# An attention and long-convolution kernel: the multiply that ends a head group goes from VectorE to GpSimd, and the table of scheduling rules is written anew

## The chip, the cores and the metric

The kernel runs on one core of one Trainium2 chip. A core has TensorE (PE, matrix multiply), VectorE (DVE), ScalarE (ACT), GpSimd (POOL) and SyncE (SP, which only issues transfers); the first four are meant when engines are spoken of. Each engine works through its own queue of instructions strictly in the order written, and waits at an instruction until the semaphores that it names have been raised by other engines or by transfers. The metric is the device time of one execution in microseconds (us). Before the change it is 719.2 us, the median of three runs (717.9, 719.2 and 720.85).

## The reference

Two independent computations stand side by side in the output.

```python
# A: multi-head attention, S = 2048 positions, D = 512, H = 32 heads of Dh = 16
qkv = (x @ wqkv) -> q, k, v per head
scores = einsum("bhqd,bhkd->bhqk", q, k) * Dh ** -0.5
p = softmax(scores, axis=-1)
o = einsum("bhqk,bhkd->bhqd", p, v)
a = o.reshape(B, S, D) @ wo
# B: a convolution over all 2048 positions, one filter per channel
kv = shift_conv(k, shift_k) * v          # 4 taps
y = causal_conv(kv, ssm_k) + kv * ssm_D  # by FFT in the reference
b = q * y
out = concatenate([a, b], axis=-1)
```

Part A has 32 x 2048 x 2048 exponentials, and these set the pace of the kernel.

## The kernel before, in words

**Tiles.** The scores are made in blocks of 128 keys by 512 queries for one head. A block is one bank of PSUM (128 x 512, 32-bit). A group `n` is 4 heads by 512 queries; there are 32 groups (0 to 31), each with 4 x 16 blocks, 2048 blocks in all. TensorE makes a block from `KTo` and `QT` (`qk_mm`, L910): a head has 16 dimensions, and four heads use four bands of 32 rows of the array at the same time.

**Two ways to an exponential.** Most blocks go to ScalarE: `emit_exp` (L935) takes 2 or 3 banks at once (128x1024 or 128x1536), applies Exp, and writes 16-bit numbers to `PT`. About a quarter goes to VectorE (`exp_on_dve`): one instruction (L1019) adds a constant to a block in PSUM and stores 16-bit integers whose bits, read as bf16, are a rough exponential; two more, on SBUF alone, make shifted copies of two blocks at a time, `near` (L1029, 128x1024) and `far` (L1036, 128x2048). The sum of the four copies, each with its own weight, is close to the exponential. TensorE forms that sum when it multiplies by the values: a ScalarE block is one matmul with `VA`, a VectorE block is four (one with `VA`, three with `VS`, the values times three weights), all at L1128, four heads side by side.

**The end of a group.** The values carry columns of ones, so that the matmuls of L1128 also give each query's sum of exponentials. When all blocks of a group have been multiplied, `finish_group` runs: VectorE transposes the bank into `DT` (L1220), takes the reciprocal of the sums (L1227, 128x16 into `DR`), multiplies the values by it into `DTN` (L1231, 16 by 16 numbers per partition), and after every second group transposes `DTN` back into `OTN` (`turn_back`, L1240), from which TensorE later forms the product with `wo` (L1294). There are 31 such multiplies; the last group goes in four quarters through `finish_last`, with small instructions on VectorE, and is not touched by the change.

**Other work.** TensorE also makes q, k and v (L583, L592, L615), the products with `wo`, and the convolution of part B as 4096 small matmuls (L1379); where it would idle, short matmuls with zeros (L1584) are put in. VectorE empties the banks of all of these. GpSimd sets up constants at the start and issues transfers: `QT` from `QS` (8 short ones for each of 15 pairs of groups), loads of `B_q`, the stores of both halves of the output. SyncE issues the loads of the filters.

**What sets the order.** The whole program is written by one Python loop that keeps a clock for each engine (`Eng.t`) with a time for each instruction (the `us=` pairs: time after the instruction before, and time after the last input). At each step it decides by these clocks what comes next: which blocks go to VectorE, whether ScalarE gets 2 or 3 banks, where matmuls of values, convolution and projections go between. Its thresholds are module constants (`LOW_2`, `MARGIN`, `LAGS` and so on), and `POLICY` changes some of them whenever about 64 more blocks have been handed out: 32 rows, the first number of each being the count of blocks. VectorE's work that may wait a little stands in lists (`flow`), of which the loop takes the item that could start first (`pick`); each item has a kind, its inputs, the function that issues it, its times, and a condition.

Of the kernel before, what the change touches and what calls it, by code (L numbers as in the profile page):

```python
# [149 lines left out]
LATE = 0.3  # L150
# [15 lines left out]
NEED = 10.0  # L166
# [1 line left out]


POLICY = (  # L170
    (0, {"DELAY": 3, "EVEN_MORE": 4, "FIRST": 2, "HALF": 0.35, "HURRY": 2, "JOIN": 0.15, "JOIN_D": 0.5, "LAGS": 16, "LATE": 0.3, "LATE_D": 0.4, "LEAD": 2, "LIN_D": 0.3, "LOW": 6.0, "LOW_2": 2.0, "LOW_A": 9.0, "LOW_L": 0.0, "MARGIN": 0.35, "MARGIN_D": 0.1, "MARGIN_P": 0.1, "MIN_L": 1, "NOW": 10, "OPEN": 40, "OVER_C": 0.1, "PRESS": 0, "PRIOR": 1, "R_LIN": 5, "SAFE": 1.0, "SOON": 0.3, "SOON_P": -0.1, "S_FX": 0.55, "TURN": 0.0}),
    (0, {"OVER_C": 0.05, "MIN_L": 2, "LIN_D": 0.0, "SAFE": 2.0}),
    (65, {"DELAY": 2, "JOIN": 0.25}),
    (194, {"LOW_2": 3.0}),
    (256, {"JOIN_D": 0.6, "EVEN_MORE": 6, "MARGIN_P": -0.3}),
    (320, {"LOW_2": 2.0, "JOIN_D": 0.5, "OVER_C": 0.1, "DELAY": 3, "EVEN_MORE": 4, "JOIN": 0.15, "MARGIN_P": 0.1, "MIN_L": 1, "LIN_D": 0.3, "SAFE": 1.0}),
    (384, {"JOIN": 0.25}),
    (448, {"PRESS": 20, "NOW": 6, "LOW": 5.5}),
    (514, {"MARGIN_P": 0.0, "OPEN": 30}),
    (578, {"LOW_2": 3.0, "PRESS": 0, "JOIN": 0.05, "MARGIN_P": 0.1, "NOW": 10, "OPEN": 40, "LOW": 6.0}),  # L180
    (640, {"PRIOR": 0, "HALF": 0.5}),
    (704, {"LOW_A": 2, "FIRST": 1}),
    (769, {"LOW_A": 9.0, "LOW_2": 2.0, "MARGIN": 0.32, "FIRST": 2, "PRIOR": 1, "JOIN": 0.15, "LEAD": 6}),
    (834, {"MARGIN": 0.35, "SOON_P": 0.1, "TURN": 0.2, "HALF": 0.35, "LEAD": 2, "SAFE": 2.0}),
    (899, {"LOW_2": 3.0, "LOW_L": 1, "MARGIN": 0.3, "R_LIN": 6, "SOON_P": -0.1, "TURN": 0.0, "SAFE": 1.0}),
    (961, {"HURRY": 0}),
    (1025, {"PRESS": 10}),
    (1090, {"LOW_2": 2.0, "LOW_L": 0.0, "LAGS": 10, "R_LIN": 5, "PRESS": 0, "HURRY": 2}),
    (1154, {"OVER_C": 0.0, "JOIN": 0.25}),
    (1218, {"MARGIN": 0.35, "OVER_C": 0.1, "LAGS": 8, "EVEN_MORE": 2, "JOIN": 0.15}),  # L190
    (1282, {"LOW_A": 5, "MARGIN_D": 0.0}),
    (1344, {"OVER_C": 0.15, "FIRST": 3, "LOW": 4.5, "SAFE": 2.0}),
    (1408, {"SOON": 0.2}),
    (1473, {"JOIN_D": 0.4, "OVER_C": 0.0}),
    (1537, {"JOIN": 0.05}),
    (1600, {"LOW_A": 2, "JOIN_D": 0.5, "MARGIN_D": 0.2, "OVER_C": 0.1, "LAGS": 16, "FIRST": 2, "EVEN_MORE": 4, "S_FX": 0.45, "JOIN": 0.15, "SOON": 0.3, "LOW": 6.0, "SAFE": 1.0}),
    (1665, {"JOIN_D": 0.7, "MARGIN": 0.3, "S_FX": 0.5, "LIN_D": 0.0}),
    (1729, {"LOW_A": 9.0, "JOIN_D": 0.5, "MARGIN_D": 0.1, "MARGIN": 0.35, "SOON_P": -0.2, "S_FX": 0.55, "LATE": 0.2, "TURN": 0.2, "LEAD": 6, "LIN_D": 0.3}),
    (1794, {"LAGS": 8, "DELAY": 4}),
    (1858, {"HURRY": 6, "JOIN": 0.05}),  # L200
    (1922, {"LAGS": 16, "HURRY": 2, "DELAY": 3, "SOON_P": -0.1, "LATE": 0.3, "JOIN": 0.15, "TURN": 0.0, "LEAD": 2, "LATE_D": 0.5}),
    (1985, {"LATE_D": 0.4}),
)


# [128 lines left out]
def bass_concat_heads__mha_block__ssm_conv_h3__prompt_kernel(  # L334
# [22 lines left out]
    def sem(name):  # L357
        return enter(nc.semaphore(name))
# [857 lines left out]
    def finish_group(n, j, h):  # L1216
        dt = DT[:, :]
        p = n // 2
        dtn = DTN[:, p % 2, :]
        h_t = urgent(lambda e: e.transpose(out=dt, in_=PS[:, PVB, :]), [h, h_mul.get(n - 1)], slack=S_T, us=(0.63, 0.751))  # L1220
        bank_free[PVB] = h_t
        blocks = dt.rearrange("p (b i) -> p b i", i=32)
        rcp = DR[:, n % 2, :].rearrange("p (b i) -> p b i", i=1)
        st = {"h": h_t}

        def recip(us):
            st["h"] = dve.op(lambda e: e.reciprocal(rcp, blocks[:, :, DH:DH + 1]), [h_t], us=us)  # L1227

        def mult(us):
            r = n % 2  # L1230
            h_mul[n] = dve.op(lambda e: e.tensor_tensor(  # L1231
                dtn.rearrange("p (b i) -> p b i", i=32)[:, :, DH * r:DH * r + DH],
                blocks[:, :, 0:DH], rcp.broadcast_to([128, 16, DH]), ALU.mult), [st["h"], h_otn.get(p - 2)], us=us)
# [428 lines left out]
    for p in sorted(pieces):  # L1662
# [4 lines left out]
        h = do_piece(*p)  # L1667
# [62 lines left out]
```

## Time and profile before

| what | value |
|---|---|
| median of 3 runs | 719.2 us |
| the profiled execution, its own time | 722.91 us |
| its span from first to last instruction | 721.1 us |
| busy in the span: ACT, DVE, PE, POOL | 703.4, 691.3, 683.2, 96.5 us |
| mean granted TensorE clock | 0.995 |
| exponentials on ScalarE | 640 instructions, 700.5 us |
| blocks on VectorE | 513 instructions, 342.6 us; their copies 2 x 257, 275.5 us |
| the multiply of the change on VectorE | 31 instructions, 12.8 us |

The profile is one execution. Busy time is the union of an engine's instructions; instructions of one engine overlap a little in the record (the next begins before the one before has ended), so what an instruction costs in a full queue is better read from the distance between two starts than from its recorded length. "Idle before, releaser" tells how long the engine stood still before an instruction and which instruction, by its semaphore, ended that; "issue" means that nothing in the profile explains it.

### The profile page before, as it was taken

The numbers are of one execution on the slowest core, as the hardware profiler recorded it, in microseconds if no ns is written. First come the engines' busy times: TensorE is split into PE (matmuls) and PEld (weight loads), VectorE is DVE, ScalarE is ACT, GpSimd is POOL, SyncE is SP. The second block draws the span as 40 slices with busy tenths as digits, with TensorE's granted clock in tenths as the row PEclk, the third lists the DMA queues.
The fourth block names the chain that finished last, engine by engine and source line by source line (L and its number), as shares of the span: only waits on it lengthen the run. The fifth ranks groups of instructions, "written<-read, shape, count | busy, mean of one in ns | idle before, by whom it ended". The sixth has DMA issues, their size and how long they took to land.

```text
span 721.1 us, 25543 instructions
## 1 busy us (share of the span) xinstructions
PE 683.2 (95%) x11264; PEld 275.0 (38%) x11264; DVE 691.3 (96%) x1313; ACT 703.4 (98%) x646; POOL 96.5 (13%) x161
## 2 busy tenths in 40 slices
PE   9999999999899999999999999999999999999988
PEld 4334334334334434434333334333333333332244
DVE  5999999999799999999999999999999999999994
ACT  7999999999799999999999999999999999999997
POOL 5200311020020201002041020100202030211001
PEclk9999999999899999999999999999999999999999
DMA  9988644778857877588987578988885874713001
GB/s 229 289 215 270 141 168 140 258 254 299 269 204 277 292 269 264 161 306 294 332 258 217 184 247 313 338 288 307 295 318 189 310 281 163 288 57 59 16 17 32
DMA packets 83045, 164.23 MB, mean 228 GB/s; under 512 B 41232, under 2 KB 47256, under 8 KB 82680
## 3 DMA queue, kind: packets, MB, share of 16 engines
q1 hardware_dynamic: 75880, 153.61, 62.4%
q0 software_dynamic: 5856, 8.66, 4.9%
q8 instruction: 90, 1.47, 0.8%
q10 hardware_dynamic: 1200, 0.33, 0.2%
q14 instruction: 19, 0.16, 0.1%
HBM read 149.17 MB, written 8.54 MB: 219 GB/s over the span
## 4 chain that ended last, share of the span: by engine, by line
ACT 49%; DVE 32%; PE 18%; issue 1%
ACT PT L935 49%; DVE RST L1019 15%; DVE RST L1036 7%; PE PS L1128 7%; PE PS L910 6%; DVE RST L1029 4%; PE PS L1379 2%; DVE YB L1395 1%; DVE DT L1220 1%; PE PS L1294 1%; DVE KV L651 1%; PE PS L583 1%; DVE VA L666 1%; DVE KTo L640 1%; DVE VS L1060 0%
## 5 line engine op out<-in xcount | busy, mean ns | idle before, releaser
L935 ACT ACTIVATE PT<-PS 128x1024 bf16<-128x1024 f32 (+1 forms) x640 | 700.5, 1266 | 8.7 <-PE PS L910 7.8
L1019 DVE TENSOR_SCALAR RST<-PS 128x512 uint16<-128x512 f32 x513 | 342.6, 679 | 4.7 <-PE PS L910 4.0
L910 PE MATMUL PS<-QT,KTo 32*128 32x512 bf16 (+2 forms) x2248 | 257.6, 365 | 30.6 <-ACT PT L935 8.4
L1128 PE MATMUL PS<-PT,VA 128*32 128x512 bf16 (+2 forms) x1696 | 279.9, 367 | 0.3 <-issue 0.2
L1128 PE MATMUL PS<-RST,VS 128*32 128x512 bf16 (+1 forms) x1656 | 242.2, 370 | 0.3
L1036 DVE TENSOR_SCALAR RST<-RST 128x2048 uint16<-128x2048 uint16 x257 | 173.9, 681 | 0.6
L910 PEld LDWEIGHTS PS<-QT,KTo 32*128 32x128 bf16 x2248 | 67.9, 91 | 215.8 <-ACT PT L935 131.9
L1128 PE MATMUL PS<-RST,VA 128*32 128x512 bf16 (+1 forms) x552 | 123.7, 372 | 0.9 <-DVE DT L1220 0.7
L429 POOL DMA_DIRECT2D QT<-QS x120 | 65.6, 555 | 432.5 <-DVE QS L631 390.5
L1029 DVE TENSOR_SCALAR RST<-RST 128x1024 uint16<-128x1024 uint16 x257 | 101.6, 415 | 0.6
L1128 PEld LDWEIGHTS PS<-PT,VA 128*32 128x32 bf16 x1696 | 68.9, 94 | 79.4 <-issue 57.1
L1379 PE MATMUL PS<-WR,KV 128*28 128x128 bf16 (+7 forms) x4096 | 99.1, 221 | 0.0
L1379 PEld LDWEIGHTS PS<-WR,KV 128*30 128x30 bf16 (+7 forms) x4096 | 77.4, 101 | 27.9 <-issue 7.4
L1128 PEld LDWEIGHTS PS<-RST,VS 128*32 128x32 bf16 x1656 | 59.1, 95 | 53.6 <-issue 31.3
L1584 PE MATMUL PS<-IDN,ZW 128*32 128x256 bf16 (+3 forms) x150 | 37.9, 301 | 0.2
L1128 PEld LDWEIGHTS PS<-RST,VA 128*32 128x32 bf16 x552 | 30.8, 95 | 14.2 <-issue 7.2
L1220 DVE STREAM_TRANSPOSE DT<-PS 128x512 f32<-128x512 f32 x31 | 22.0, 709 | 3.8 <-PE PS L1128 3.5
L1395 DVE CAST YB<-PS 128x512 bf16<-128x512 f32 x32 | 21.8, 680 | 1.4 <-PE PS L1379 0.8
L429 POOL DMA_DIRECT2D out_dram<-OUTA x15 | 11.4, 759 | 62.5 <-DVE OUTA L1302 62.5
L1294 PE MATMUL PS<-WKV,OTN 128*128 128x512 bf16 (+1 forms) x68 | 18.9, 371 | 0.3 <-DVE OTN L1269 0.3
L615 PE MATMUL PS<-WKV,xT 128*128 128x128 bf16 x256 | 18.6, 220 | 0.5 <-DVE KTo L640 0.4
L592 PE MATMUL PS<-xT,WKV 128*128 128x512 bf16 (+1 forms) x64 | 16.7, 376 | 0.4
(72 smaller groups left out, 252.1 us busy)
## 6 DMA issues: line engine op xcount, KB each, us to landing
WR<-kz_scratch SPq DMA_DIRECT2D x256, 528.0 KB, 6.2
kz_scratch<-WR SPq DMA_DIRECT2D x4, 544.0 KB, 4.7
kt_scratch<-in_B_k_dram SPq DMA_DIRECT2D x1, 2048.0 KB
QN<-in_B_q_dram POOLq DMA_DIRECT2D x4, 512.0 KB, 7.0
out_dram<-QN POOLq DMA_DIRECT2D x4, 512.0 KB, 6.9
QT<-QS POOLq DMA_DIRECT2D x120, 16.0 KB, 3.4
out_dram<-OUTA POOLq DMA_DIRECT2D x15, 128.0 KB, 2.2
QN<-in_B_ssm_k_dram SPq DMA_DIRECT2D x1, 1024.0 KB, 8.2
```

Source lines behind the costliest of these rows:

```text
L429: f(outp, inp).then_inc(dsem.sem, 16)
L910: ins = e.matmul(PS[:, bank, i * w:i * w + w], lhsT=KTo[32 * s:32 * s + 32, OF[n_] % 2, kt * 128:(kt + 1) * 128], rhs=QT[32 * s:32 * s + 3 ...
L935: h_exp[T] = act.op(lambda e: e.activation(PT[:, p0:p0 + n, :].rearrange("p b f -> p (b f)"), PS[:, banks[0]:banks[0] + n, :].rearrange("p ...
L1019: st["h"].append(urgent(lambda e: e.tensor_scalar(lin[:, 0, half, :].bitcast(U16), PS[:, bank, :], FIX_ADD, FIX_HI, ALU.add, ALU.min), [h, ...
L1029: st["s"][0] = dve.op(lambda e: e.tensor_scalar(both(lin, 1, 2).bitcast(U16), both(lin, 0, 1).bitcast(U16), SHIFTS[0], None, ALU.add), [st ...
L1036: st["s"][1] = dve.op(lambda e: e.tensor_scalar(both(dst, 0, 2).bitcast(U16), both(lin, 0, 2).bitcast(U16), SHIFTS[1], None, ALU.add), [st ...
L1128: ins = e.matmul(dst, lhsT=w, rhs=rhs, start=first, stop=last, tile_position=(0, 32 * s))
L1220: h_t = urgent(lambda e: e.transpose(out=dt, in_=PS[:, PVB, :]), [h, h_mul.get(n - 1)], slack=S_T, us=(0.63, 0.751))
L1294: ins = e.matmul(PS[:, b, c0:c1], lhsT=OTN[:, PAIRS.index((o, qb)), t * 128:(t + 1) * 128], rhs=WO[:, o, c0:c1], start=(o == 0), stop=(o = ...
L1379: ins = e.matmul(dst, lhsT=KV[:, channel(qd) // 4, 2 * n:2 * NB, g], rhs=WR[:, (2 * qd + g // 2) % (R_W), w0:w0 + 128], start=(n == 0), st ...
L1395: bank_free[BGB] = h_ybw[0] = urgent(lambda e: e.tensor_copy(YB[:, qd % 8 // 4, :], src), [h, h_yb[0]], slack=S_C, us=V512)
L1584: pe.op(lambda e, s=s, dst=dst, rhs=rhs, rows=rows, first=first: e.matmul(dst, lhsT=ZW[:, 0:rows], rhs=rhs, start=first, stop=first, tile_ ...
```

## The change

The multiply of `finish_group` is issued on GpSimd instead of VectorE. Reciprocal and multiply, two items of the list before, become one item `scale`, which issues the reciprocal on VectorE and the multiply on GpSimd; the item waits for the same condition that the multiply had. As `DR` has two halves and is now read by another engine, the reciprocal of group `n` also waits for the multiply of group `n - 2`. `turn_back` now waits for GpSimd. The loop counts the multiply as 0.5 us on GpSimd, done 0.7 us after the reciprocal.

```diff
-        st = {"h": h_t}
-
-        def recip(us):
-            st["h"] = dve.op(lambda e: e.reciprocal(rcp, blocks[:, :, DH:DH + 1]), [h_t], us=us)
-
-        def mult(us):
+        def scale(us):
             r = n % 2
-            h_mul[n] = dve.op(lambda e: e.tensor_tensor(
+            h_r = dve.op(lambda e: e.reciprocal(rcp, blocks[:, :, DH:DH + 1]), [h_t, h_mul.get(n - 2)], us=us)
+            h_mul[n] = pool.op(lambda e: e.tensor_tensor(
                 dtn.rearrange("p (b i) -> p b i", i=32)[:, :, DH * r:DH * r + DH],
-                blocks[:, :, 0:DH], rcp.broadcast_to([128, 16, DH]), ALU.mult), [st["h"], h_otn.get(p - 2)], us=us)
+                blocks[:, :, 0:DH], rcp.broadcast_to([128, 16, DH]), ALU.mult), [h_r, h_otn.get(p - 2)], us=(0.5, 0.7))
...
-        u_r, u_m, u_t = (0.155, 0.28), (0.334, 0.46), (0.6, 0.75)
-        flow.insert(0, [("n", lambda: [h_t], recip, u_r, lambda: True),
-                        ("n", lambda: [st["h"]], mult, u_m, lambda: p < 2 or p - 2 in h_otn)])
+        u_t = (0.6, 0.75)
+        flow.insert(0, [("n", lambda: [h_t], scale, (0.155, 0.28), lambda: p < 2 or p - 2 in h_otn)])
```

All 32 rows of `POLICY` are replaced, two of them for example:

```diff
-    (194, {"LOW_2": 3.0}),
-    (961, {"HURRY": 0}),
+    (258, {"S_FX": 0.6}),
+    (960, {"PRIOR": 0}),
```

Since the loop decides by its clocks, both edits together give another order on all engines. Counted over the whole program: ScalarE has 640 exponentials as before, but 248 instead of 255 of three banks and 392 instead of 385 of two. VectorE has 520 instead of 513 blocks, and 260 instead of 256 full pairs of `near` and `far` (a single one with half the width is gone). TensorE has 18 more full-width matmuls with values of VectorE's blocks and 12 more narrow ones. SyncE's queue has the same rows, except that three loads of the filter now stand behind a copy of `KV` and a load of `B_v`.

The first place is VectorE at the end of group 13 (of the groups 0 to 31), from the transpose into `DT` to the transpose back into `OTN`. Before:

```order
L1220 STREAM_TRANSPOSE DT<-PS 128x512
L1019 TENSOR_SCALAR RST<-PS 128x512 x2
L1227 RECIPROCAL DR<-DT 128x16
L1036 TENSOR_SCALAR RST<-RST 128x2048
L1231 TENSOR_TENSOR DTN<-DT,DR 128x16x16
L1029 TENSOR_SCALAR RST<-RST 128x1024
L1240 STREAM_TRANSPOSE OTN<-DTN 128x512
L1019 TENSOR_SCALAR RST<-PS 128x512
```

and now:

```order
L1219 STREAM_TRANSPOSE DT<-PS 128x512
L1018 TENSOR_SCALAR RST<-PS 128x512
L1225 RECIPROCAL DR<-DT 128x16
L1035 TENSOR_SCALAR RST<-RST 128x2048
L1028 TENSOR_SCALAR RST<-RST 128x1024
L1235 STREAM_TRANSPOSE OTN<-DTN 128x512
L1018 TENSOR_SCALAR RST<-PS 128x512
```

The multiply is gone from VectorE, and only `far` and `near` stand between the reciprocal and the transpose back, which needs the multiply from GpSimd. After 27 of the 31 reciprocals the next instruction is one that works on SBUF alone (`near`, `far`, a scaling of values or a copy).

The second place is GpSimd's queue from the end of its set-up to about a quarter of the program (`QT<-QS` are the short transfers of q, `QN<-in_B_q` the loads of `B_q`). Before:

```order
L709 AFFINE_SELECT OTN<-SHK 128x2048
L429 DMA QT<-QS 16x512 x8
L429 DMA QN<-in_B_q_dram 64x32x128 x2
L429 DMA QT<-QS 16x512 x56
L429 DMA out_dram<-QN 64x32x128 x2
```

and now:

```order
L708 AFFINE_SELECT OTN<-SHK 128x2048
L428 DMA QT<-QS 16x512 x8
L1226 TENSOR_TENSOR DTN<-DT,DR 128x16x16 x2
L428 DMA QN<-in_B_q_dram 64x32x128 x2
L428 DMA QT<-QS 16x512 x8
L1226 TENSOR_TENSOR DTN<-DT,DR 128x16x16
L428 DMA QT<-QS 16x512 x8
```

The 31 multiplies stand between the transfers that GpSimd issues, and each waits there for VectorE's reciprocal.

More of the change, by code (lines that the diff above doesn't have):

```diff
@@ L173 @@
-    (65, {"DELAY": 2, "JOIN": 0.25}),
-    (194, {"LOW_2": 3.0}),
[L175 to L185, printed above, removed]
-    (961, {"HURRY": 0}),
-    (1025, {"PRESS": 10}),
-    (1090, {"LOW_2": 2.0, "LOW_L": 0.0, "LAGS": 10, "R_LIN": 5, "PRESS": 0, "HURRY": 2}),
@@ L189 @@
[L189 to L202, printed above, removed]
+    (0, {"DELAY": 3, "EVEN_MORE": 4, "FIRST": 2, "HALF": 0.35, "HOT": 20, "HURRY": 2, "JOIN": 0.15, "JOIN_D": 0.5, "LAGS": 16, "LATE": 0.3, "LATE_D": 0.4, "LIN_D": 0.3, "LOW_2": 2.0, "LOW_A": 9.0, "LOW_L": 0.0, "MARGIN": 0.35, "MARGIN_P": 0.1, "MIN_L": 1, "NEED": 10.0, "OPEN": 40, "OVER_C": 0.1, "PRIOR": 1, "PV_ON": 3, "PV_WANT": 3, "R_LIN": 5, "S_FX": 0.55}),
@@ new lines @@
+    (0, {"MARGIN": 0.32, "MARGIN_P": -0.1}),
+    (65, {"MARGIN": 0.35, "S_FX": 0.5, "MARGIN_P": 0.1}),
+    (129, {"PRIOR": 2, "DELAY": 4, "MARGIN_P": -0.3}),
+    (192, {"PRIOR": 1, "DELAY": 3, "S_FX": 0.55, "MARGIN_P": 0.1}),
+    (258, {"S_FX": 0.6}),
+    (321, {"JOIN_D": 0.4, "OVER_C": 0.2, "S_FX": 0.55}),
+    (384, {"JOIN_D": 0.5, "OVER_C": 0.1}),
+    (450, {"MARGIN": 0.32, "HALF": 0.5}),
+    (512, {"MARGIN": 0.35, "HALF": 0.35}),
+    (640, {"LOW_2": 2.2, "LAGS": 8}),
+    (706, {"PV_ON": 1, "HURRY": 6}),
@@ new lines @@
+    (769, {"LOW_2": 2.0, "LAGS": 16, "PV_ON": 3, "HURRY": 2}),
+    (898, {"LOW_2": 2.5, "HOT": 4}),
+    (960, {"PRIOR": 0}),
+    (1024, {"LOW_L": 3, "HALF": 0.2, "NEED": 12.0}),
+    (1089, {"LOW_L": 1, "MARGIN": 0.32, "LAGS": 10, "OPEN": 50}),
+    (1154, {"LOW_2": 2.0, "LOW_L": 0.0, "MARGIN": 0.35, "LAGS": 16, "PRIOR": 1, "LATE": 0.2, "HALF": 0.35, "OPEN": 40, "HOT": 20, "NEED": 10.0}),
+    (1217, {"LOW_2": 2.2, "R_LIN": 6, "LIN_D": 0.0}),
+    (1282, {"LOW_2": 2.0, "R_LIN": 5, "LATE": 0.3, "LIN_D": 0.3}),
@@ new lines @@
+    (1345, {"HOT": 10}),
+    (1409, {"HOT": 20}),
+    (1473, {"LOW_2": 3.0, "MARGIN": 0.32, "JOIN": 0.05}),
+    (1536, {"LOW_2": 2.5}),
+    (1600, {"MARGIN": 0.3}),
+    (1664, {"PV_ON": 2}),
+    (1729, {"OVER_C": 0.15, "FIRST": 3, "LATE_D": 0.3}),
+    (1793, {"EVEN_MORE": 6}),
+    (1858, {"LOW_A": 2, "LATE_D": 0.5, "OPEN": 30}),
+    (1923, {"PV_WANT": 2, "R_LIN": 4, "MIN_L": 2}),
+    (1985, {"LOW_A": 9.0, "LOW_2": 2.0, "MARGIN": 0.35, "OVER_C": 0.1, "FIRST": 2, "PV_ON": 3, "PV_WANT": 3, "R_LIN": 5, "EVEN_MORE": 4, "JOIN": 0.15, "MIN_L": 1, "LATE_D": 0.4, "OPEN": 40}),
```

2 lines of the change are left out of this document (removed).

## The prediction, made before the changed kernel was run

> **What bounds the kernel now.** I read the page's head first, then the stretches of 80 us, then the groups of instructions with their shapes kept apart, then the timeline at the places that these pointed to.
>
> ```profile
> span 721.1 us, 25543 instructions
> PE 683.2 (95%) x11264; PEld 275.0 (38%) x11264; DVE 691.3 (96%) x1313; ACT 703.4 (98%) x646; POOL 96.5 (13%) x161
> ACT 49%; DVE 32%; PE 18%; issue 1%
> 80.00:160.00 80.00, 77.19 (x1260) 30.61 (x1259) 79.54 (x151) 79.83 (x74) 11.60 (x22) 1.00 0.59 197
> 160.00:240.00 80.00, 75.78 (x1274) 31.32 (x1270) 74.45 (x141) 75.52 (x71) 6.97 (x13) 0.96 0.78 275
> 400.00:480.00 80.00, 76.46 (x1369) 30.72 (x1366) 79.03 (x148) 79.96 (x75) 9.47 (x17) 1.00 0.77 265
> ```
>
> The last three rows are stretches: length, then busy time of PE, PE's weight loads, DVE, ACT and POOL, the granted clock, the share of the transfer engines, GB/s. ScalarE and VectorE are both full (79.83 and 79.54 of 80), TensorE has 3 us to spare in 80, and the chain of the end runs through all three. So ScalarE's exponentials set the pace as long as VectorE and TensorE are on time, and VectorE has no room to be late. One stretch differs, 160 to 240:
>
> ```profile
> 189.00 0.60 PE L910 MATMUL PS<-QT,KTo 32*128 32x512 bf16 x1 [1.78 <-issue]
> 189.64 1.45 ACT L935 ACTIVATE PT<-PS 128x1536 bf16<-128x1536 f32 x1 [1.95 <-PE PS L910]
> 191.26 0.45 DVE L1060 TENSOR_SCALAR VS<-VA 128x1264 bf16<-128x1264 bf16 x1
> 192.13 1.02 ACT L935 ACTIVATE PT<-PS 128x1024 bf16<-128x1024 f32 x1 [1.04 <-PE PS L910]
> 195.26 3.71 ACT L935 ACTIVATE PT<-PS 128x1536 bf16<-128x1536 f32 x3 [0.51 <-PE PS L910]
> ```
>
> TensorE stands still for 1.78 us with nothing shown as the reason, its matmuls take 0.60 us afterwards, and ScalarE loses 1.95 + 1.04 + 0.51 = 3.5 us. The profiled execution took 722.91 us (1.8 around its span of 721.1), 3.7 above the median of the runs; without this stall it would be 719.4. I take the stall as belonging to this execution, and 719.2 as the base.
>
> **The change part by part.** The prices:
>
> ```profile
> L935 ACT ACTIVATE PT<-PS 128x1024 bf16<-128x1024 f32 x385 | 395.5, 1101 | 2.3 <-PE PS L910 2.1
> L935 ACT ACTIVATE PT<-PS 128x1536 bf16<-128x1536 f32 x255 | 382.9, 1516 | 6.4 <-PE PS L910 5.7
> L1029 DVE TENSOR_SCALAR RST<-RST 128x1024 uint16<-128x1024 uint16 x256 | 101.3, 415 | 0.6
> 282.31 0.23 DVE L1227 RECIPROCAL DR<-DT 128x16 f32<-128x16 f32 x1
> 282.46 0.36 DVE L1029 TENSOR_SCALAR RST<-RST 128x1024 uint16<-128x1024 uint16 x1
> 282.74 0.41 DVE L1231 TENSOR_TENSOR DTN<-DT,DR 128x256 bf16<-128x256 f32 x1
> 283.07 0.69 DVE L1036 TENSOR_SCALAR RST<-RST 128x2048 uint16<-128x2048 uint16 x1
> 283.67 0.69 DVE L1019 TENSOR_SCALAR RST<-PS 128x512 uint16<-128x512 f32 x1
> 284.27 0.68 DVE L631 TENSOR_SCALAR QS<-PS 128x512 bf16<-128x512 f32 x1
> ```
>
> *ScalarE.* Seven exponentials shrink from three banks to two: 7 x (1516 - 1101 ns) = 2.9 us less, on the path. 719.2 - 2.9 = 716.3.
>
> *VectorE.* From start to start the multiply costs 283.07 - 282.74 = 0.33 us, so 31 of them free 10.2 us. Added are 7 blocks at 0.60 (283.67 to 284.27), 4 `far` at 0.60 (283.07 to 283.67) and 4 `near` at 0.28 (282.46 to 282.74) to 0.41 (the group's mean), say 0.35: 4.2 + 2.4 + 1.4 = 8.0. Net 2.2 us freed.
>
> *TensorE.* 18 more full-width matmuls, four side by side, are 4.5 more steps of less than 0.6 us (the slow one above), under 2.7 us; the 3 us idle in each 80 hide them. If that cover went, they would cost that.
>
> *GpSimd's multiply.* The trace has no such instruction. The nearest rows:
>
> ```profile
> L709 POOL TENSOR_SCALAR_AFFINE_SELECT OTN<-SHK 128x2048 bf16<-128x2048 bf16 x1 | 2.0, 2012 | 7.1 <-DMA SHK<-in_B_shift_k_dram 7.1
> L535 POOL COPY IDP<-IDN 128x128 bf16<-128x128 bf16 x1 | 0.4, 388 | 0.1
> L532 POOL TENSOR_SCALAR_AFFINE_SELECT IDN<-IDN 128x128 bf16<-128x128 bf16 x1 | 0.3, 282 | 0.2 <-POOL IDN L531 0.2
> ```
>
> The two selects give (2012 - 282) / 1920 = 0.90 ns an element on a base of 0.17 us. For 256 elements that is 0.40 us with one input, and 0.63 if the two inputs are read in turn; with the copy's (388 - 170) / 128 = 1.7 ns for each of two, 1.05. I take 0.63, the select being the only row with a length to check it: 31 x 0.63 = 19.5 us on an engine that is busy 13%. [...]
>
> *What the multiply does to VectorE.* GpSimd's long transfers show that the two engines get in each other's way:
>
> ```profile
> 73.92 2.21 POOL L429 DMA_DIRECT2D QN<-in_B_q_dram  x2 [37.70 <-PE PS L604]
> 75.74 0.91 DVE L1036 TENSOR_SCALAR RST<-RST 128x2048 uint16<-128x2048 uint16 x1
> 77.94 1.02 ACT L935 ACTIVATE PT<-PS 128x1024 bf16<-128x1024 f32 x1 [0.24 <-PE PS L910]
> 368.42 2.25 POOL L429 DMA_DIRECT2D out_dram<-QN  x2 [40.03 <-DVE QN L1413]
> 368.80 1.04 DVE L1060 TENSOR_SCALAR VS<-VA 128x1264 bf16<-128x1264 bf16 x1
> 371.91 1.45 ACT L935 ACTIVATE PT<-PS 128x1536 bf16<-128x1536 f32 x1 [0.33 <-PE PS L910]
> 377.95 2.68 POOL L429 DMA_DIRECT2D QN<-in_B_q_dram  x2 [0.48 <-DMA out_dram<-QN]
> 379.94 1.27 DVE L1029 TENSOR_SCALAR RST<-RST 128x1024 uint16<-128x1024 uint16 x2
> 382.91 1.02 ACT L935 ACTIVATE PT<-PS 128x1024 bf16<-128x1024 f32 x1 [0.34 <-PE PS L910]
> 656.78 2.23 POOL L429 DMA_DIRECT2D out_dram<-QN  x2 [13.47 <-DVE QN L1413]
> 658.20 1.32 DVE L1036 TENSOR_SCALAR RST<-RST 128x2048 uint16<-128x2048 uint16 x1
> ```
>
> While GpSimd works, `far` takes 0.91 and 1.32 instead of 0.69, the scaling of values 1.04 instead of 0.45 (at 191.26), two `near` 1.27 instead of about 0.75: 0.22 + 0.63 + 0.59 + 0.52 = 2.0 us late in 9.4 us of GpSimd's work (2.21 + 2.25 + 2.68 + 2.23), 0.21 for each. And 2 to 3 us later ScalarE stands still for 0.24, 0.33 and 0.34 us (after 658.20 it does not): 0.91 us, or 0.46 of VectorE's lateness. All four are instructions on SBUF alone; those that read PSUM keep their length. So the multiply delays VectorE by X, and ScalarE by 0.46 X. The lower end is X = 0: GpSimd may be the one that waits. The upper is 31 x 0.63 = 19.5, every multiply stopping a `near` or `far` throughout. By the rate of the four places X = 0.21 x 19.5 = 4.1, which I take, since their mixture of instructions is that of the new places.
>
> [...]
>
> *The transpose back* is one wait more. In group 13 only `far` and `near` cover it: 0.60 + 0.28 = 0.88 us, against 0.69 for `far` (if GpSimd must let it finish) + 0.63 = 1.32, some 0.45 late. Groups 5, 11 and 21 have one of the two and one block: 0.2 to 0.3 late each. Together 1.1 us; the other 11 have more between. Behind the waiting transpose stand blocks whose banks TensorE needs, so I add it to X: 5.2 us. The reciprocal's new wait looks back two groups, some 44 us (721.1 / 32 each), and costs nothing even if the multiply stands behind a transfer that waits; the same for q's transfers, which stand at most 0.63 us behind a multiply. SyncE's queue keeps its order but for three loads.
>
> **The sum.** 719.2 - 2.9 + 0.46 x (5.2 - 2.2) = 717.7. With X = 0: 715.3. With X = 19.5 + 1.1 = 20.6: 724.8.
>
> **The rivals.**
> 1. *Gain in full.* GpSimd waits rather than VectorE, and VectorE's 2.2 us make the transfers of banks earlier: 715.3, and 714 if some of ScalarE's 5 us of idle time outside the stall (2.3 + 6.4 - 3.5) goes too. For it: nearly every multiply is ready just when VectorE has begun an SBUF instruction, and the block that follows reads PSUM. Against it: in eight groups two or more SBUF instructions stand in a row.
> 2. [...] Each multiply stops VectorE for its length: 724.8; at 1.05 us a multiply more still. It is slower than 722.8 from X = 6.5 / 0.46 + 2.2 = 16.3 us on, 0.53 us a multiply. For it: the rows above, where VectorE lost up to 0.63 at once. Against it: only 4 of 8 such transfers did that.
> 3. *TensorE's unexplained stall.* The new order has its matmuls at other places against the loads. One stall like that at 189 in every run makes 717.7 + 3.5 = 721.2, two 724.7. For it: it is in the profile once; against it: the median seems to be without.
> 4. *The change does nothing to the pace*: ScalarE keeps its idle time and loses only work, 716.3, which lies within my own case.
>
> **How the numbers follow.** 0.5% is 3.6 us, about what a measurement of this kernel tells from no change: faster is below 715.6, slower above 722.8. My case (with rival 4) has 0.40, mostly inside (0.06 faster, 0.30 same, 0.04 slower); rival 1 0.27 (0.24 faster, 0.03 same); rival 2 0.17 (0.03 same, 0.14 slower); rival 3 0.16 (0.06 same, 0.10 slower). Faster 0.30, same 0.42, slower 0.28. My case alone spans 715.3 to 721; the range takes in 714 of rival 1 with half a us, and the 724.8 of rivals 2 and 3: 713.5 to 725.5.
>
> **What would show it.** Right: ScalarE's exponentials busy near 697.6 us; 31 multiplies on GpSimd of about 0.6 us; some `near` and `far` behind reciprocals of 0.9 to 1.3 us, in all about 4 us above their usual length; about 1 us of VectorE's idle time before the transpose back; ScalarE's idle time before exponentials at 5 us and 1 to 2 more. Wrong: no lengthened `near` or `far` (rival 1), lengthened ones at nearly every group (rival 2), a TensorE stall of over 1.5 us without releaser (rival 3), or multiplies well over 1 us with long waits before the transposes back.

## The result and the profile after

The changed kernel takes 723.69 us (median of 4 runs, 723.13 to 724.0), against 719.17 for the kernel before on the same chip: a ratio of 1.0059, 95% interval 1.0041 to 1.0076. It is slower, by 4.5 us; 717.7 had been forecast, with more weight on "no change" and on "faster" than on this. Two runs of the experiments below are left out as slow, one of e8_before_relieved (946.28 us, at a granted clock of 0.557) and one of e9_before_pool (1639.7 us, at 1.0); no trace shows why.

The page of the kernel after, head, chain and two of its groups:

```profile
span 721.4 us, 25642 instructions
PE 681.5 (94%) x11302; PEld 276.3 (38%) x11302; DVE 693.4 (96%) x1295; ACT 703.0 (97%) x646; POOL 121.0 (17%) x192
DVE 42%; ACT 30%; PE 23%; POOL 2%; issue 2%; DMA 1%; SPq 1%
L1035 DVE TENSOR_SCALAR RST<-RST 128x2048 uint16<-128x2048 uint16 x260 | 178.9, 693 | 1.0
L1226 POOL TENSOR_TENSOR DTN<-DT,DR 128x256 bf16<-128x256 f32 x31 | 23.5, 757 | 321.9 <-DVE DR L1225 321.7
```

VectorE lost 31 multiplies and is busier than before, 693.4 us against 691.3; the chain that ended last now runs mostly through VectorE (42%, before 32%) and less through ScalarE (30%, before 49%). The profiled execution took 723.13 us.

Its groups with shapes kept apart (the first two on ScalarE, then VectorE):

```profile
L934 ACT ACTIVATE PT<-PS 128x1024 bf16<-128x1024 f32 x392 | 398.3, 1075 | 4.2 <-PE PS L909 3.2
L934 ACT ACTIVATE PT<-PS 128x1536 bf16<-128x1536 f32 x248 | 369.5, 1505 | 4.2 <-PE PS L909 3.1
L1028 DVE TENSOR_SCALAR RST<-RST 128x1024 uint16<-128x1024 uint16 x260 | 107.3, 430 | 0.8
L1235 DVE STREAM_TRANSPOSE OTN<-DTN 128x512 bf16<-128x512 bf16 x15 | 10.6, 704 | 1.5 <-POOL DTN L1226 1.5
```

Before, `far` was

```profile
L1036 DVE TENSOR_SCALAR RST<-RST 128x2048 uint16<-128x2048 uint16 x256 | 173.4, 682 | 0.6
```

`near` rose from 415 to 430 ns in the mean and `far` from 682 to 693, and the transposes back wait 1.5 us in all for GpSimd's multiply. The tile `DTN` in the trace after gives the shortest, the middle and the longest multiply:

```profile
L1226 POOL TENSOR_TENSOR DTN<-DT,DR x31: 613/670/1017, 38.6 to 695.4; 128x256 bf16<-128x256 f32 x31
```

How the two engines meet is seen at the end of group 13, in the timeline of VectorE and of GpSimd after (start, length, engine, line):

```profile
323.65 0.24 DVE L1225 RECIPROCAL DR<-DT 128x16 f32<-128x16 f32 x1
323.80 0.64 DVE L1035 TENSOR_SCALAR RST<-RST 128x2048 uint16<-128x2048 uint16 x1
324.35 0.85 DVE L1028 TENSOR_SCALAR RST<-RST 128x1024 uint16<-128x1024 uint16 x1
325.12 0.70 DVE L1235 STREAM_TRANSPOSE OTN<-DTN 128x512 bf16<-128x512 bf16 x1
...
328.71 0.41 DVE L1028 TENSOR_SCALAR RST<-RST 128x1024 uint16<-128x1024 uint16 x1
...
323.97 0.94 POOL L1226 TENSOR_TENSOR DTN<-DT,DR 128x256 bf16<-128x256 f32 x1 [20.15 <-DVE DR L1225]
```

The multiply begins 0.08 us after the reciprocal has ended, while `far` runs; it takes 0.94 instead of 0.62 us, which fits that it stands still for most of the 0.47 us until `far` ends (324.44). Then `near` takes 0.85 instead of 0.42, which fits that it stands still while the multiply runs. So both engines lose here: the multiply 0.32 us beside a running SBUF instruction of VectorE, and the next one of VectorE 0.43 us beside the multiply. Over the whole trace, `near`, `far` and the scalings of values that overlap a multiply are 4.1 us longer than their usual length (14 instructions), and those that overlap a transfer issued by GpSimd 1.7 us (before: 2.0). What decides is the second instruction behind the reciprocal. In 20 groups the multiply comes when one on SBUF alone has just begun, and it is the multiply that becomes longer (0.66 to 0.94 us). Where a second one on SBUF alone follows, in eight of the 20, that one is held up by 0.30 to 0.43 us (in seven it is among the 14, in one it is a copy); in the other twelve the second reads PSUM and takes 0.68 to 0.69 us, as elsewhere (0.68 in the middle), and VectorE loses nothing.

The 1.5 us of waits have another cause. They stem from groups 3, 7 and 25, whose multiply stands in GpSimd's queue behind eight q transfers, and starts 3.1 to 5.0 us behind the reciprocal; the longest, in VectorE's timeline:

```profile
589.83 0.71 DVE L1235 STREAM_TRANSPOSE OTN<-DTN 128x512 bf16<-128x512 bf16 x1 [0.78 <-POOL DTN L1226]
```

### The profile page after: what moved, and what is told of

The parts are those of the page before. It is cut to its first block, busy times and chain, and to the rows that moved or that the text cites. A ratio compares the mean times of both kernels' runs of the same rounds, so it can differ in the third digit from the quotient of the medians.

```text
span 721.4 us, 25642 instructions
## 1 busy us (share of the span) xinstructions
PE 681.5 (94%) x11302; PEld 276.3 (38%) x11302; DVE 693.4 (96%) x1295; ACT 703.0 (97%) x646; POOL 121.0 (17%) x192
## 3 DMA queue, kind: packets, MB, share of 16 engines
q8 instruction: 90, 1.47, 0.8%
## 4 chain that ended last, share of the span: by engine, by line
DVE 42%; ACT 30%; PE 23%; POOL 2%; issue 2%; DMA 1%; SPq 1%
ACT PT L934 30%; DVE RST L1018 19%; DVE RST L1035 9%; PE PS L1127 9%; PE PS L909 7%; DVE RST L1028 5%; PE PS L1373 2%; POOL QT L428 2%; DVE DT L1219 2%; PE PS L1288 2%; DVE YB L1389 1%; DVE OTN L1235 1%; PE PS L603 1%; DMA xT<-in_A_x_dram 1%; SPq L428 1%
## 5 line engine op out<-in xcount | busy, mean ns | idle before, releaser
L1018 DVE TENSOR_SCALAR RST<-PS 128x512 uint16<-128x512 f32 x520 | 348.2, 682 | 3.1 <-PE PS L909 2.4
L1127 PE MATMUL PS<-PT,VA 128*32 128x512 bf16 (+2 forms) x1686 | 275.5, 366 | 1.0 <-DVE VA L665 0.8
L1035 DVE TENSOR_SCALAR RST<-RST 128x2048 uint16<-128x2048 uint16 x260 | 178.9, 693 | 1.0
L1127 PE MATMUL PS<-RST,VA 128*32 128x512 bf16 (+1 forms) x562 | 126.2, 369 | 1.1 <-DVE DT L1219 0.8
L1028 DVE TENSOR_SCALAR RST<-RST 128x1024 uint16<-128x1024 uint16 x260 | 107.3, 430 | 0.8
L1373 PE MATMUL PS<-WR,KV 128*30 128x128 bf16 (+7 forms) x4096 | 97.0, 220 | 0.3 <-issue 0.3
L1373 PEld LDWEIGHTS PS<-WR,KV 128*26 128x26 bf16 (+7 forms) x4096 | 77.4, 101 | 26.2 <-issue 4.0
L1226 POOL TENSOR_TENSOR DTN<-DT,DR 128x256 bf16<-128x256 f32 x31 | 23.5, 757 | 321.9 <-DVE DR L1225 321.7
L1578 PE MATMUL PS<-IDN,ZW 128*32 128x128 bf16 (+3 forms) x158 | 34.9, 294 | 0.2
```

Source lines behind the costliest of these rows:

```text
L1018: st["h"].append(urgent(lambda e: e.tensor_scalar(lin[:, 0, half, :].bitcast(U16), PS[:, bank, :], FIX_ADD, FIX_HI, ALU.add, ALU.min), [h, ...
L1028: st["s"][0] = dve.op(lambda e: e.tensor_scalar(both(lin, 1, 2).bitcast(U16), both(lin, 0, 1).bitcast(U16), SHIFTS[0], None, ALU.add), [st ...
L1035: st["s"][1] = dve.op(lambda e: e.tensor_scalar(both(dst, 0, 2).bitcast(U16), both(lin, 0, 2).bitcast(U16), SHIFTS[1], None, ALU.add), [st ...
L1127: ins = e.matmul(dst, lhsT=w, rhs=rhs, start=first, stop=last, tile_position=(0, 32 * s))
L1373: ins = e.matmul(dst, lhsT=KV[:, channel(qd) // 4, 2 * n:2 * NB, g], rhs=WR[:, (2 * qd + g // 2) % (R_W), w0:w0 + 128], start=(n == 0), st ...
L1578: pe.op(lambda e, s=s, dst=dst, rhs=rhs, rows=rows, first=first: e.matmul(dst, lhsT=ZW[:, 0:rows], rhs=rhs, start=first, stop=first, tile_ ...
```

## The experiments

Each time is a median, set against the kernel before on the same chip (719.17 us for after; 719.52 for e3 to e6, 719.7 for e7 to e10, 719.31 for e11, e12, e1 and e2). e1 and e2 rest on two runs each, e9 on three.

| run | what it is | us | ratio to before, 95% interval |
|---|---|---|---|
| after | the change | 723.69 | 1.0041 to 1.0076 |
| e3_short | after, GpSimd multiplies a sixteenth from group 4 on | 719.45 | 0.997 to 1.0013 |
| e4_extra | before, GpSimd multiplies as well | 725.83 | 1.005 to 1.0103 |
| e5_twice | after, GpSimd multiplies twice | 736.78 | 1.0192 to 1.029 |
| e6_on_vector | after, the multiply on VectorE | 732.7 | 1.0147 to 1.0216 |
| e7_short_relieved | e3_short, shorter transposes | 720.25 | 0.9994 to 1.0032 |
| e8_before_relieved | before, shorter transposes | 719.18 | 0.9983 to 1.0012 |
| e9_before_pool | before, the multiply on GpSimd | 731.07 | 1.0134 to 1.0199 |
| e10_after_wait | after, the multiply waits past the copies | 722.97 | 1.0041 to 1.008 |
| e11_relieved | after, 40 `far` halved | 721.68 | 1.0005 to 1.0032 |
| e12_before_pool_first | e9_before_pool, the multiply ahead of the transfers | 721.15 | 1.001 to 1.004 |
| e1_before_new_table | before, the new table | 732.99 | 1.0163 to 1.0203 |
| e2_pool_old_table | after, the old table | 733.19 | 1.0165 to 1.0206 |

### More and less of the multiply

```diff
+            m = 16 if n < 4 else 1
-                dtn.rearrange("p (b i) -> p b i", i=32)[:, :, DH * r:DH * r + DH],
-                blocks[:, :, 0:DH], rcp.broadcast_to([128, 16, DH]), ALU.mult), [h_r, h_otn.get(p - 2)], us=(0.5, 0.7))
+                dtn.rearrange("p (b i) -> p b i", i=32)[:, 0:m, DH * r:DH * r + DH],
+                blocks[:, 0:m, 0:DH], rcp[:, 0:m, :].broadcast_to([128, m, DH]), ALU.mult), [h_r, h_otn.get(p - 2)], us=(0.5, 0.7))
```

> Leaves out most of the normalization: from group 4 on, GpSimd multiplies only the first 16 of 256 numbers per partition; the order on every engine is that of the changed kernel. Theory A (GpSimd's multiply holds VectorE up, 4.1 us of longer shifts and 1.5 us of waits before the transposes back, and ScalarE follows): most of both goes, 718 to 720 us. Theory B (the new order has ScalarE wait at places of its own, with or without GpSimd): 722.5 to 724 us, about as the changed kernel's 723.7.

```diff
+            h_extra[n] = pool.op(lambda e: e.tensor_tensor(
+                EXTRA[:, :].rearrange("p (b i) -> p b i", i=DH),
+                blocks[:, :, 0:DH], rcp.broadcast_to([128, 16, DH]), ALU.mult), [st["h"]], us=(0.0, 0.0))
```

> The kernel before in its own order, its multiply still on VectorE, and besides GpSimd makes the same multiply into a tile that nobody reads. Theory A: VectorE's shifts become longer by about 4 us in all, and the time rises from 719.2 to 721 (at 0.46 for each) or 723 (at one for one). Theory B: the longer shifts are absorbed, 719 to 720 us.

```diff
+            def twice(e):
+                for dst in (EXTRA[:, :].rearrange("p (b i) -> p b i", i=DH), dtn.rearrange("p (b i) -> p b i", i=32)[:, :, DH * r:DH * r + DH]):
+                    ins = e.tensor_tensor(dst, blocks[:, :, 0:DH], rcp.broadcast_to([128, 16, DH]), ALU.mult)
+                return ins
+            h_mul[n] = pool.op(twice, [h_r, h_otn.get(p - 2)], us=(0.5, 0.7))
```

> The changed kernel in its order, with every multiply made twice on GpSimd (once into a tile that nobody reads), so that GpSimd is at it for about 1.3 us instead of 0.65 and the transposes back wait longer. Theory A: the lengthened shifts and the waits about double, 5.6 us more for VectorE, 727 to 730 us. Theory B: 724 to 725 us.

```diff
-            h_mul[n] = pool.op(lambda e: e.tensor_tensor(
+            kept = dve.t
+            h_mul[n] = dve.op(lambda e: e.tensor_tensor(
...
+            dve.t = kept
+            pool.t = max(pool.t + 0.5, at(h_r, h_otn.get(p - 2)) + 0.7)
```

> The changed kernel's order, with the multiply back on VectorE directly behind the reciprocal, which the loop's clocks are not told of. VectorE gets 31 x 0.33 = 10.2 us of work, and loses the 4.1 us of longer shifts and 1.5 us of waits: 4.6 us net. Theory A, one for one: 728 us; at 0.46: 726 us. Theory B (VectorE's lateness matters little, the order is what costs): 723 to 725 us.

All three kernels derived from the one after keep its order on every engine. The same place in the timeline of VectorE of e3_short, where GpSimd's multiply is short:

```profile
321.33 0.23 DVE L1225 RECIPROCAL DR<-DT 128x16 f32<-128x16 f32 x1
321.49 0.63 DVE L1035 TENSOR_SCALAR RST<-RST 128x2048 uint16<-128x2048 uint16 x1
322.03 0.43 DVE L1028 TENSOR_SCALAR RST<-RST 128x1024 uint16<-128x1024 uint16 x1
322.38 0.70 DVE L1236 STREAM_TRANSPOSE OTN<-DTN 128x512 bf16<-128x512 bf16 x1
...
325.98 0.41 DVE L1028 TENSOR_SCALAR RST<-RST 128x1024 uint16<-128x1024 uint16 x1
```

From the reciprocal to the transpose back it is 1.05 us here and 1.47 after. The difference, 0.42, is still there at the last row, 3.6 us later: after runs 2.32 us behind e3_short at the reciprocal, 2.74 at the transpose back, 2.73 at the last row. Since both have the same 1295 instructions in one order on VectorE, this can be done for all of them. At the first reciprocal after is 0.9 us behind; from there on it falls 4.2 us further behind within the eight instructions behind the reciprocals, and in all the rest of the program it gains 2.3, of which 2.1 stem from two groups in which e3_short's TensorE itself stood still. So hardly anything is made up again.

The waits of the transposes back in the trace of e5_twice (us in all, times, longest):

```profile
DVE OTN L1238 <- POOL DTN L1229: 6.7, 10, 1.4
```

and VectorE's own multiply in e4_extra, which has both its inputs in SBUF as GpSimd's has:

```profile
L1236 DVE TENSOR_TENSOR DTN<-DT,DR x31: 407/417/875, 38.5 to 696.8; 128x256 bf16<-128x256 f32 x31
```

It, too, stands still behind GpSimd (875 instead of 407 ns); its 31 take 18.1 us instead of 12.8. The lateness of VectorE in each trace is the sum of what its `near`, `far` and scalings are above their usual length, of its waits for the multiply, and of the multiply itself where it is there:

| step | change of VectorE's lateness | change of the time |
|---|---|---|
| after to e3_short | -3.9 (copies), -0.9 (waits) = -4.8 | -4.6 |
| after to e5_twice | +5.9 (copies), +5.2 (waits) = +11.1 | +12.8 |
| after to e6_on_vector | +13.9 (31 x 0.45: the multiply, and 0.11 later start behind the reciprocal), -4.8 (copies), -1.5 (waits) = +7.6 | +8.7 |
| before to e4_extra | +5.3 (its multiply), +0.7 (copies) = +6.0 | +6.3 |

(Times as differences to the kernel before: after +4.5, e3_short -0.1, e5_twice +17.3, e6_on_vector +13.2, e4_extra +6.3.) Some of these runs had a lowered granted clock (0.992 to 0.998): three of four of e4_extra and of e6_on_vector, two of e5_twice. The runs at 0.999 or more alone, against such runs of before on that chip (719.03 in the middle), give -4.1 for the step to e3_short (ten runs), +11.3 to e5_twice (two), +7.4 to e6_on_vector (one) and +4.8 to e4_extra (one). So VectorE's lateness comes through at 0.8 to 1.0 of its length, about in full. The theory by which ScalarE loses 0.46 of it falls. e4, e5 and e6 all took longer than either theory had expected: what VectorE's own multiply lost behind GpSimd's (5.3 us), the waits of e5_twice (5.2) and the 0.45 for 0.33 us in e6_on_vector had been left out or set too low.

### Relief for VectorE elsewhere

```diff
-        h_t = urgent(lambda e: e.transpose(out=dt, in_=PS[:, PVB, :]), [h, h_mul.get(n - 1)], slack=S_T, us=(0.63, 0.751))
+        w = 512 if n == 0 else 128
+        h_t = urgent(lambda e: e.transpose(out=DT[:, 0:w], in_=PS[:, PVB, 0:w]), [h, h_mul.get(n - 1)], slack=S_T, us=(0.63, 0.751))
```

The same edit was made in e3_short and in before.

> The order of the changed kernel with the shortened multiply on GpSimd (as in the first experiment), and from group 1 on VectorE transposes only 128 of 512 columns into DT; so three quarters of the values and sums are stale. That takes about 30 x 0.43 = 13 us from VectorE, in the same order on every engine. Theory V (VectorE sets the pace in this order, about one for one): from 719.5 to 706 to 713 us, until ScalarE or TensorE stops the fall. Theory S (ScalarE's waits lie in the order, whatever VectorE does): 718 to 719.5 us.

> The kernel before in its own order, with the same cut: from group 1 on VectorE transposes only 128 of 512 columns into DT, the rest is stale; 13 us less for VectorE. Theory V: 709 to 714 us. If ScalarE then sets the pace in this and in the run beside it, this one is 2.9 us slower than that one, by the seven exponentials of three banks that are of two there. Theory S: 718 to 719.5 us.

```diff
+            cut = j >= 16 and j % 6 == 3 and n == 2
+            out, src = (dst[:, 0:2, 0, :], lin[:, 0:2, 0, :]) if cut else (both(dst, 0, 2), both(lin, 0, 2))
-            st["s"][1] = dve.op(lambda e: e.tensor_scalar(both(dst, 0, 2).bitcast(U16), both(lin, 0, 2).bitcast(U16), SHIFTS[1], None, ALU.add),
+            st["s"][1] = dve.op(lambda e: e.tensor_scalar(out.bitcast(U16), src.bitcast(U16), SHIFTS[1], None, ALU.add),
```

> The changed kernel with its order and its full multiply on GpSimd; but in 40 of the 260 pairs of blocks (one in six from pair 16 on, away from the ends of the groups) the step that adds the far bits (VectorE, line 1035) handles only the first block of the pair, 128x2x512 instead of 128x2048 numbers, and the rest of the tile keeps what an earlier pair left there, so that the result is not the reference's. About 0.26 us each and 10 us in all less for VectorE, at other places than the multiply. Theory 'no room to recover': a late shift costs the time because VectorE, 96 per cent busy, can't catch up afterwards; with room it catches up and most of the 4.5 us come back: 719.5 to 720.5. Theory 'on the spot': each late shift holds up ScalarE and TensorE at once, and room elsewhere doesn't help: 722.5 to 724.

Busy times of e8_before_relieved, from its page:

```profile
PE 675.2 (94%) x11231; PEld 274.6 (38%) x11264; DVE 683.6 (95%) x1313; ACT 703.0 (98%) x646; POOL 96.0 (13%) x161
```

VectorE has 7.7 us less than before (13 had been expected), and the time is the same (0.9983 to 1.0012). Set against the trace of before, instruction by instruction, the shorter transposes bring VectorE forward by some 5.3 us over the groups, and it loses 4.8 of that again within the eight instructions behind the reciprocals, mostly waiting for TensorE's blocks (the stretch about 189 us left out). e7_short_relieved gains nothing over e3_short either. So lateness of VectorE costs about its full length here, but time given to VectorE alone is worth nothing here when it is on time. ScalarE, busy for 703.0 us of a span of 717.3, probably sets the pace then; that it isn't TensorE, busy for 94%, was not tried. e11_relieved stands between its two theories: with 11 us of relief in the kernel after, where VectorE is late, 2.1 of the 4.5 us come back. (33 of its 40 shortened `far` lie more than eight instructions behind a reciprocal, seven nearer.) Against the trace of after, its instructions gain 2.0 us away from the ends of groups. So a late VectorE caught up a part here when it had room; in the kernel after, where it is busy for 96% of the span, it has next to none.

### Other places for the multiply

e9_before_pool takes before's order, gives the multiply to GpSimd and nothing else to VectorE, and lets the multiply wait for the end of the copies that stand directly behind the reciprocal. e10_after_wait does the same waiting in the kernel after. e12_before_pool_first also moves the multiply ahead of the q transfers in GpSimd's queue.

```diff
+        last = max([v for s, v in waits if s is dve.sem], default=0)
+        while last + 1 in shifts:
+            last += 1
+        if last + 1 not in turns:
+            pool.ops[i] = ([(s, last if s is dve.sem else v) for s, v in waits], fn, sm)
```

> The kernel before in its own order on every engine (same blocks on VectorE, 513, same exponentials), with the multiply issued on GpSimd at the place of the reciprocal, and waiting there until VectorE is through with the shifts that follow the reciprocal; the freed time is given to no other work. VectorE loses 10.2 us of work and gets 1 to 3 us of longer shifts and waits. Theory V: 710 to 714 us, faster than both kernels. Theory S: 718 to 720 us.

> The changed kernel in its order; GpSimd's multiply waits not for the reciprocal but for the end of the shifts that VectorE does directly behind it, so that it runs beside blocks that VectorE reads from PSUM. Of the 4.1 us of longer shifts about 3 go. Theory V: 720.5 to 721.5 us; Theory S: 723 to 724 us.

```diff
+            if at_recip - seen[0] <= 20:
+                waits = [(s, v) for s, v in pool.ops[i][0] if s is not dve.sem] + [(dve.sem, max(mine + [at_recip]))]
+                pool.ops[k:i + 1] = [(waits, *pool.ops[i][1:])] + pool.ops[k:i]
```

> The kernel before in its own order with the multiply on GpSimd and nothing given to VectorE in its place, as in the run e9_before_pool; but the multiply now stands in GpSimd's queue ahead of the eight small q transfers that were issued just before it. The waits ahead of the transposes back (9.7 us there) should fall to 1 to 2 us. VectorE is relieved of 10.2 us by the 31 multiplies. Theory 'relief is worth nothing, lateness counts in full': 719 to 720.5. Theory 'VectorE sets the pace': 711 to 714.

The timeline of GpSimd and VectorE in e9_before_pool:

```profile
588.88 1.98 POOL L429 DMA_DIRECT2D QT<-QS  x4 [21.03 <-DVE DR L1243]
592.33 1.93 POOL L429 DMA_DIRECT2D QT<-QS  x4 [1.46 <-issue]
594.27 0.63 POOL L1236 TENSOR_TENSOR DTN<-DT,DR 128x256 bf16<-128x256 f32 x1
...
588.51 0.24 DVE L1243 RECIPROCAL DR<-DT 128x16 f32<-128x16 f32 x1
594.93 0.71 DVE L1259 STREAM_TRANSPOSE OTN<-DTN 128x512 bf16<-128x512 bf16 x1 [4.83 <-POOL DTN L1236]
```

The multiply, whose inputs are ready at 588.75, stands behind eight transfers of 0.49 us each and a pause, and VectorE waits 4.83 us at the transpose back; this is the longest of six waits, 9.7 us in all. Neither theory had seen that: 731.07 is above both. Behind three of these waits TensorE stood idle for 1.7, 1.7 and 4.6 us, and after the last two of these the granted clock was one half for 3.4 and 6.8 us, which is in the time as well: all three runs have a clock of 0.993 to 0.995. With the multiply first, the tile `DTN` of e12_before_pool_first shows multiplies at rest:

```profile
L1237 POOL TENSOR_TENSOR DTN<-DT,DR x31: 612/618/944, 39.9 to 694.3; 128x256 bf16<-128x256 f32 x31
```

Only one is above 0.64 us, the waits fall to 0.3 us and the lengthened copies to 0.6. Yet it takes 721.15, not 719 to 720.5, though VectorE is 6.3 us less busy than before. Eight of its ten runs have a mean granted clock of 0.998 or less, and with such a clock before takes 720.4 to 724.8 (see "What was right" below); the other two, at 0.999, took 718.57 and 720.57. Its TensorE stalls where that of before did in its profiled execution (last section). What the multiply itself costs there can't be told from this; that 6.3 us of relief bring no gain, as in e8_before_relieved, can.

In e10_after_wait the multiplies are at rest as well (620 ns in the middle), the lengthening falls from 4.1 to 2.1 us, the waits stay at 1.5, and the time falls by 1.2, less than theory V has and more than theory S. Its profile has two stalls of TensorE (1.3 and 1.4 us) that the one of after doesn't have, so whether the whole 2 us came back can't be told.

### Each edit alone

e1_before_new_table is before with the new `POLICY`, e2_pool_old_table after with the old one.

> The kernel before with nothing changed but the table of rules, which is the changed kernel's (the multiply stays on VectorE). Theory 'each table fits its own place of the multiply': an order that leaves waits, several us slower than before, 725 to 733. Theory 'the table alone brings the loss': 723 to 724.

> The changed kernel with the table of rules of the kernel before (the multiply on GpSimd as in the change). Theory 'each table fits its own place of the multiply': several us slower than before, 725 to 733. Theory 'the table alone brings the loss, GpSimd's multiply none': 718 to 720.

The exponentials in the pages of e1_before_new_table and of e2_pool_old_table:

```profile
L934 ACT ACTIVATE PT<-PS 128x1536 bf16<-128x1536 f32 (+1 forms) x636 | 701.4, 1272 | 12.8 <-PE PS L909 12.0
```

```profile
L935 ACT ACTIVATE PT<-PS 128x1024 bf16<-128x1024 f32 (+1 forms) x641 | 700.8, 1242 | 16.8 <-PE PS L910 15.6
```

Each edit alone costs 13.7 to 13.9 us, both together 4.5. A table fits the work that it was made for: ScalarE waits longer, mostly for TensorE (12.8 and 16.8 us, after 8.4), with the other one. What in the order makes these waits was not followed. "The table alone" and "the multiply alone" are therefore no shares into which 4.5 could be split; e3_short, which leaves the order as it is, tells what the multiply costs in the order after.

## Why the prediction was wrong, point by point

**What was right, and what came out right by luck.** The multiply's price, 0.63 us, measured 0.61 to 0.62 at rest. That GpSimd's work lengthens VectorE's SBUF instructions: 14 beside multiplies, by 4.1 us in all. The base: of 54 runs of the kernel before, 45 had a granted clock of 0.999 or more, with a median of 719.28, and nine a lower one, with 720.4 to 724.8; the stall at 189, if the lowered clock is its mark, belongs to few runs, as I had taken it. That X = 4.1 was forecast and 4.1 measured is luck in the size: my rate came from the four of eight transfers that had lengthened something, and was laid on all 31 multiplies; in the trace after most of the loss lies where a second SBUF instruction meets a multiply. That condition stands in my first rival, with its eight groups, and would have been the one to count by. The waits before the transposes back, 1.1 forecast and 1.5 measured, are luck as well: none is at groups 5, 11, 13 and 21, where I had them. In group 13 the transpose back starts 0.21 us after the multiply's end, since the lengthened `near` had already made it late, so that I had counted the same delay twice. The 1.5 us are at multiplies that stand behind q transfers, which I had put at nothing; I had looked only at transfers that stand behind a multiply.

**The step that failed: "0.46 of VectorE's lateness".** I had this from four places where ScalarE showed 0.91 us of idle time after 2.0 us of lateness. The runs that change the lateness alone show 0.8 to 1.0 in its place. Idle time shows too little, since ScalarE's records overlap in a full queue: behind idle time an exponential is recorded with 1.02 us (two banks) or 1.45 (three), in the full queue with up to 1.33 and 1.76. I take the difference as time for which it stood ready behind the one before. The trace of before shows it already: at my four places the distances between two starts on ScalarE are 0.37, 0.57 and 0.46 us above their least, and nothing at the fourth, 1.4 us of 2.0 where idle time shows 0.91. The mean length of an exponential fell from 1101 and 1516 ns before to 1075 and 1505 after, and in e5_twice further, without any change of work:

```profile
L935 ACT ACTIVATE PT<-PS 128x1024 bf16<-128x1024 f32 x392 | 393.6, 1053 | 7.5 <-PE PS L910 6.4
L935 ACT ACTIVATE PT<-PS 128x1536 bf16<-128x1536 f32 x248 | 364.4, 1480 | 10.0 <-PE PS L910 8.5
```

The distance between two starts on ScalarE is never below 0.90 us after a two-bank exponential and 1.33 after a three-bank one; what the distances have above that sums to 18.1 us before (without the stall), 23.6 after and 36.1 in e5_twice. From after to e5_twice that is 12.5, of which idle time shows 9.1. Two signs that I had named for "right" failed accordingly: ScalarE's exponentials are busy for 700.0 us and not 697.6, and its idle time before them is 8.4 us and not 6 to 7.

**The credit for "2.2 us freed" on VectorE.** I let it balance the lateness. With 4.8 us of lateness in copies and waits taken away, e3_short is at 719.45, no better than before; and e7, e8 and e12 show that 6 to 8 us less work on VectorE bring nothing where it isn't late. So a saving at one place did not pay here for a delay at another; the order is fixed and the engines meet in every group.

**The "2.9 us less" on ScalarE.** The work did fall, by least distances 7 x 0.43 = 3.0 us. But e3_short, which has that order and little lateness, is level with before. Two things that take it back can be read in the traces; they were not tried apart. The program's end, behind the last exponential, became longer by 0.7 us, as the last row of exponentials in the timeline of each shows, of before and of after (start and length; spans 721.1 and 721.4):

```profile
711.20 4.92 ACT L935 ACTIVATE PT<-PS 128x1024 bf16<-128x1024 f32 x5
```

```profile
711.80 3.90 ACT L934 ACTIVATE PT<-PS 128x1024 bf16<-128x1024 f32 x4
```

And the starts in e3_short have 21.7 us above their least distance; less some 2 us for two stalls of TensorE (1.17 and 0.79), it is 1.6 more than in before. Together 0.7 + 1.6 = 2.3 of 3.0; the cause of the 1.6 stays open.

With 1 for 0.46, and without the two credits, my own terms give 719.2 + 4.1 + 1.1 = 724.4; measured 723.69. Of the 6.7 us by which this is above my 717.7, the factor makes 2.8 (0.54 x 5.2), the credit on VectorE 1.0 (0.46 x 2.2) and that on ScalarE 2.9, so the last is as large as the first. Of the rivals, the second is right in that multiplies hold VectorE up, though nothing here shows what in the chip makes one engine wait for the other; but "each multiply stops VectorE for its length", the condition that I had set for a slower kernel, is not needed: 4.1 us of 19.5 suffice. Of "gain in full", GpSimd does wait, in 20 groups; but VectorE loses time in eight of them, and e8_before_relieved shows that relief of VectorE brings no gain. "Nothing to the pace" falls with e3_short, which stands at 719.45 and not at 716.3. A TensorE stall is not in the profile of after, and all its four runs have a granted clock of 1.0.

## What to carry to other kernels

When two engines are both full and the order is fixed, price a change by each engine's own account: in this kernel a delay on VectorE counted about in full (0.8 to 1.0 of its length), and a saving of 6 to 8 us on VectorE alone for nothing. Before an operation goes to GpSimd, look at the next two instructions on VectorE: if both work on SBUF alone, GpSimd waited here for the first and then held up the second (by 0.30 to 0.43 us, in eight groups); if the second read PSUM, VectorE lost nothing (twelve groups). And if VectorE needs the result soon, look at what stands ahead in GpSimd's queue: with eight transfers there, VectorE waited up to 4.83 us in e9_before_pool. None of the versions tried beats the kernel before.

## What was not expected of the hardware

**A TensorE stall at one place, and the clock after it.** The timeline of TensorE in e12_before_pool_first and stretches of 1 us there (length, busy time of PE, PE's weight loads, DVE, ACT and POOL, granted clock, share of the transfer engines, GB/s):

```profile
189.03 0.39 PE L911 MATMUL PS<-QT,KTo 32*128 32x512 bf16 x1 [1.69 <-issue]
```

```profile
186.00:187.00 1.00, 1.00 (x29) 0.39 (x21) 1.00 (x4) 1.00 (x2) 0.00 (x0) 1.00 0.39 84
187.00:188.00 1.00, 0.34 (x2) 0.04 (x2) 0.67 (x2) 0.81 (x1) 0.00 (x0) 1.00 0.17 25
188.00:189.00 1.00, 0.00 (x0) 0.00 (x0) 0.00 (x0) 0.00 (x0) 0.00 (x0) 1.00 0.94 208
...
190.00:191.00 1.00, 1.00 (x31) 0.46 (x23) 1.00 (x2) 0.90 (x1) 0.00 (x0) 0.70 0.97 245
191.00:192.00 1.00, 1.00 (x10) 0.27 (x9) 1.00 (x3) 0.95 (x1) 0.00 (x0) 0.50 0.81 275
```

TensorE stands still at the same matmul as in before (1.78 us there). The transfers almost stop at first (25 GB/s) and are back (208) before TensorE is. The clock goes to one half for 3.4 us here and 6.8 in before. e8 and e9 stalled there for 0.96 and 1.15 us and kept the clock, e4's profile has no such stall. The order of after has its own places, at 450 to 474, 535, 695 and 709 us, in some executions (0.8 to 2.1 us in e3, e5, e6, e10 and e11; none above 0.4 us in the profiles of after and e7). What stops TensorE there was not found. Idle times of 1.7 to 2.1 us were followed by a lower clock: 1.78 in before and 1.69 in e12 by one half, 2.11 and 1.75 in e6 by a mean of 0.91 in the 20 us around each. Length alone doesn't decide it: of two idle times of 1.67 and 1.66 us in e9, at 243 and 548 us, only the second was followed by half the clock.

**What stays open.** e7_short_relieved, with less work than before on ScalarE and on VectorE, has a profiled execution of 718.18 but a median of 720.25 (718.18 to 724.19). Stalls of TensorE may make that spread, but this is not shown: its one profile, of the fastest run, has none above 0.4 us, and the slower runs left no profile.
